# All output products in seven block products for eight, raw products on quarters of the array, one ring of PSUM banks, and a new order of the steps

## The chip, the cores and the metric

The kernel runs on one core of one Trainium2 chip. The metric is the device time of one execution in microseconds; a smaller number is better. Five engines work side by side on their own queues: TensorE (PE in the profile, with its weight loads as PEld), VectorE (DVE), ScalarE (ACT), GpSimd (POOL) and SyncE (SP, which here only issues transfers). Each works through its own instructions in order and waits for semaphores of the others. TensorE writes its results to PSUM, a memory of eight banks that hold 128 x 512 numbers of four bytes each; VectorE and ScalarE carry them on.

## The reference

There are 8 batches, 8 heads, 576 tokens and a head size of 64, so that the heads side by side make 512 channels. First comes an attention without softmax, whose result is normalised over each head; then a gated unit whose gate is a causal convolution over five tokens.

```python
kv = np.einsum('bhsd,bhse->bhde', k, v)
out = np.einsum('bhsd,bhde->bhse', q, kv)
rms = np.sqrt(np.mean(out * out, axis=-1, keepdims=True) + 1e-06)
x = (out / rms * g_norm)                  # then (B,H,S,D) -> (B, S, H*D)
...
for k in range(5):
    gate_pre += conv_w[k] * xp[:, k:k + S, :]     # xp: x with four rows of zeros ahead
gate = 1.0 / (1.0 + np.exp(-gate_pre))
val = x @ w_val
return (gate * val @ w_out).astype(np.float32)
```

The three weights `w_val`, `conv_w` and `w_out` arrive as 64-bit numbers; the rest has 32 bits. All products on TensorE are in 32 bits, and each of them appears in the profile as two instructions ("passes").

## The kernel before

The program is written as small functions ("steps"), and a long string `PLAN` says in which order they are recorded: "raw_pair 3 1; keep_out 0 2; ...". Each step records its instructions on one engine, and since every engine works in order, this string fixes the order on every engine's queue and on the queues of transfers. Semaphores are put in between by the recording layer.

For each batch b the steps are these; a chunk c is 128 tokens, with four whole chunks and a tail of 64 (c = 4).

- **k^T v.** `load_half` brings k and v, `kv_product` (L431) multiplies them in 64 x 64 quarters of the array, four at a time, `kv_copy` (L443, ScalarE) puts the result as blocks on the diagonal of `kv_bd`, 128 x 128 for each pair of heads, the rest of which is zero.
- **q.** For batches 0 and 1 `turn_q_rows` transposes q on TensorE and `sort_q` copies it on ScalarE; later ones are transposed in blocks of 32 x 32 by VectorE (`turn_q`).
- **Raw products.** `raw_product` (L483) multiplies whole tiles of 128 with `kv_bd` for batches 0 and 1 and for all tails; `raw_pair` (L500) takes two whole chunks of batches 2 to 7 in quarters of 64 x 64.
- **Normalising.** `square` (L524, ScalarE), `sums` (L533, VectorE), `powers` (L543, GpSimd, to the power −1/2). For two chunks of batch 0 `roots` (L550) computes the root on VectorE by Newton steps. `normalise` (L564) multiplies: on VectorE for batch 0, on ScalarE, head by head, for the others.
- **x transposed.** Batches 0 and 1 and the tails: `turn_x` on TensorE, `keep_x` on ScalarE. Whole chunks of later batches: `turn_blocks` on VectorE, then `move_blocks`, four transfers each from GpSimd's queue. `halo` on GpSimd copies the four earlier tokens for the convolution.
- **Gate.** For each quarter of the channels `gate_start` (ScalarE), four times `gate_tap` (L623, VectorE), `gate_end` (sigmoid, ScalarE).
- **Values.** Batches 0 and 1 by `val_product` (four products of 288 tokens). From batch 2 on by `val_fast`: a product of two by two blocks in seven block products in place of eight, with sums of blocks of x (`x_sums`) and of weights (`val_sums`) made by VectorE, and `val_keep` to put the parts together. `gated` (L648, VectorE) multiplies by the gate.
- **Output.** Two batches go together as i = b // 2. Batches 0 to 3 (i = 0, 1) go by `out_product` (L712): four products of 128 tokens by 512 columns for each chunk, then `keep_out` (ScalarE). Batches 4 to 7 (i = 2, 3) go by seven block products for each pair p of chunks: `token_sums` (L743) and `weight_sums` make sums of blocks on VectorE, `fast_product` (L761) multiplies (128 tokens by 256 columns, two products each), `fast_keep` (L788) adds the parts up, four copies on ScalarE and three additions on VectorE. `store` sends 128 tokens out in four transfers. All tails go by `out_product` (c = 8).
- **Weights.** `stage_weight` loads, and `narrow_weight` makes 32 bits out of 64 in eight operations, five on VectorE and three on ScalarE.

`start_warm` and `keep_warm` are products whose results nobody reads. PSUM is divided up (L238 to L245): two banks `raws` for k^T v and for most raw products, one bank "tp" for transposes, five banks "mm" for the rest; near the end `raws` is given up for two banks "ends".

Of the kernel before, what the change touches and what calls it, by code (L numbers as in the profile page):

```python
# [9 lines left out]
FP32 = mybir.dt.float32  # L10
# [5 lines left out]
P = 128  # L16
# [3 lines left out]
load_q_rows 0 1; stage_weight cw 0; load_q_rows 0 0; load_half v 0 0; load_half k 0 0; load_half v 0 1;  # L20
load_half k 0 1; warm_up; stage_weight wval 1; stage_weight wval 0; start_warm 36; turn_q_rows 0 0;
turn_q_rows 0 1; narrow_weight cw 0 0; turn_q_rows 0 2; narrow_weight cw 0 1; narrow_weight cw 0 2; sort_q 0 0;
turn_q_rows 0 3; sort_q 0 1; turn_q_rows 0 4; narrow_weight cw 0 3; kv_product 0 0; sort_q 0 2;
load_q_rows 1 0; narrow_weight cw 0 4; narrow_weight cw 0 5; load_half k 1 0; sort_q 0 3; narrow_weight cw 0 6;
load_half v 1 0; narrow_weight cw 0 7; sort_q 0 4; load_q_rows 1 1; load_half k 1 1; stage_weight wval 2;
keep_warm 2; kv_product 0 1; stage_weight wval 3; turn_cw; load_half v 1 1; kv_copy 0; keep_cw;
narrow_weight wval 1 0; raw_product 0 3; load_half v 2 0; raw_product 0 2; square 0 3; raw_product 0 4;
sums 0 3; stage_weight wout 0; square 0 2; raw_product 0 1; square 0 4; powers 0 3; sums 0 2;
narrow_weight wval 1 1; sums 0 4; raw_product 0 0; load_half v 2 1; square 0 1; narrow_weight wval 0 0;
narrow_weight wval 0 1; powers 0 2; square 0 0; normalise 0 3; sums 0 1; turn_x 0 3; sums 0 0; keep_x 0 3;  # L30
powers 0 4; normalise 0 2; narrow_weight wval 1 2; narrow_weight wval 1 3; turn_x 0 2; normalise 0 4;
turn_q_rows 1 0; roots 0; keep_x 0 2; narrow_weight wval 0 2; turn_x 0 4; sort_q 1 0; turn_q_rows 1 1;
keep_x 0 4; narrow_weight wval 0 3; normalise 0 1; turn_q_rows 1 2; halo 0; sort_q 1 1; normalise 0 0;
turn_x 0 1; narrow_weight wval 1 4; kv_product 1 0; narrow_weight wval 0 4; keep_x 0 1; sort_q 1 2;
narrow_weight wval 0 5; turn_x 0 0; narrow_weight wval 1 5; narrow_weight wval 0 6; turn_q_rows 1 3;
keep_x 0 0; narrow_weight wval 0 7; gate_start 0 0; turn_q_rows 1 4; narrow_weight wval 1 6; kv_product 1 1;
sort_q 1 3; load_q 2 0; narrow_weight wval 1 7; gate_start 0 1; narrow_weight wval 2 0; val_product 0 0 1;
gate_start 0 2; narrow_weight wval 3 0; sort_q 1 4; load_q 2 1; gate_tap 0 2 3; kv_copy 1; gate_tap 0 0 3;
narrow_weight wval 3 1; raw_product 1 3; narrow_weight wval 2 1; gate_tap 0 1 3; load_half k 2 0;
raw_product 1 2; keep_val 0 0 1; gate_tap 0 0 2; square 1 3; narrow_weight wval 3 2; val_product 0 1 1;  # L40
sums 1 3; square 1 2; gate_tap 0 1 2; powers 1 3; narrow_weight wval 2 2; load_half k 2 1; gate_tap 0 2 2;
narrow_weight wval 2 3; stage_weight wout 2; raw_product 1 1; sums 1 2; narrow_weight wval 3 3;
narrow_weight wval 2 4; raw_product 1 0; keep_val 0 1 1; powers 1 2; square 1 1; narrow_weight wval 2 5;
normalise 1 3; val_product 0 0 0; load_q 2 2; gate_tap 0 0 1; sums 1 1; turn_q 2 0; normalise 1 2; powers 1 1;
turn_x 1 3; narrow_weight wval 3 4; val_product 0 1 0; narrow_weight wval 2 6; keep_x 1 3; load_q 2 3;
narrow_weight wval 3 5; square 1 0; narrow_weight wval 2 7; normalise 1 1; turn_x 1 2; sums 1 0;
raw_product 1 4; gate_tap 0 2 1; stage_weight wout 1; powers 1 0; kv_product 2 0; narrow_weight wout 0 0;
square 1 4; sums 1 4; narrow_weight wout 0 1; narrow_weight wval 3 6; kv_product 2 1; keep_x 1 2; turn_q 2 1;
powers 1 4; normalise 1 0; gate_tap 0 2 0; turn_x 1 1; load_q 3 0; val_product 0 2 1; narrow_weight wval 3 7;
keep_x 1 1; gate_tap 0 1 1; keep_val 0 1 0; narrow_weight wout 0 2; gate_tap 0 1 0; keep_val 0 0 0; turn_x 1 0;  # L50
normalise 1 4; gate_tap 0 0 0; val_product 0 2 0; narrow_weight wout 2 0; narrow_weight wout 0 3; keep_x 1 0;
narrow_weight wout 0 4; kv_copy 2; val_product 0 3 1; turn_q 2 2; keep_val 0 2 1; keep_val 0 2 0; turn_q 2 3;
narrow_weight wout 2 1; load_q 3 1; gate_end 0 0; narrow_weight wout 0 5; turn_x 1 4; narrow_weight wout 0 6;
raw_pair 2 3; keep_val 0 3 1; keep_x 1 4; gated 0 0; narrow_weight wout 2 2; stage_weight wout 3; halo 1;
val_product 1 0 1; narrow_weight wout 0 7; load_q 3 2; square 2 3; square 2 2; sums 2 3;
narrow_weight wout 2 3; sums 2 2; powers 2 3; gate_end 0 1; val_product 1 0 0; narrow_weight wout 1 0;
gate_end 0 2; narrow_weight wout 2 4; gate_start 0 3; gated 0 1; keep_val 1 0 1; narrow_weight wout 2 5;
# [802 lines left out]
```

## Time and profile before

| | before |
|---|---|
| time, median of 3 runs | 313.97 us (313.96 to 314.11) |
| span of the profiled execution | 313.7 us |
| TensorE busy | 302.8 us, 97% |
| VectorE busy | 255.7 us, 82% |
| ScalarE busy | 191.1 us, 61% |
| GpSimd busy | 133.4 us, 43% |
| read from HBM, written | 39.21 MB, 9.44 MB |
| output products of 512 columns, whole chunks (L718) | 128 passes, of 592 ns each |
| gate taps (L625) | 128, of 810 ns each |

The profiled execution's span lies 0.3 us under the median time, so sums made against the span stand for the time with 0.3 us added. A row of the profile names the engine, the line, the operation, what is written from what, how many there are and how long they were busy; "idle before" is how long the engine stood idle ahead of them, with the instruction that ended the wait. Products are pipelined: one of 592 ns starts 429 ns after the one before, and two rows of busy time can overlap. In the chain of what ended last and in the timeline the first number is the start and the second the time taken, in microseconds.

### The profile page before, as it was taken

What the parts mean: (1) busy time and instruction counts of PE and PEld (TensorE: products, weight loads), DVE (VectorE), ACT (ScalarE), POOL (GpSimd) and SP (SyncE); (2) the same over time, 40 slices, a digit from 0 to 9 for tenths busy, and PEclk for the clock granted to TensorE, in tenths of its full rate; (3) what the DMA queues carried; (4) which work ended last, traced back from release to release, by engine and by line L of the source; (5) the groups of instructions that cost most, each with busy time, mean ns of one, the idle gap of its engine ahead of it and who ended that gap; (6) DMA issues with size and microseconds to landing.
All of it is one profiled execution on the core that took longest, in us unless ns stands there. A gap on an engine that the chain in (4) does not pass through costs nothing.

```text
span 313.7 us, 8362 instructions
## 1 busy us (share of the span) xinstructions
PE 302.8 (97%) x3197; PEld 217.6 (69%) x3197; DVE 255.7 (82%) x462; ACT 191.1 (61%) x542; POOL 133.4 (43%) x175
## 2 busy tenths in 40 slices
PE   7978999999999999999999999999999999999993
PEld 7866878777645485757666776587668868888582
DVE  1149899999999969899999899899998999764412
ACT  1457899999485867747685858485773343352120
POOL 3033073435588456666684659265749000000000
PEclk9999999999999999999999999999999999999999
DMA  7999597599677769668966986422335213022322
GB/s 276 377 386 352 149 294 219 173 298 239 186 189 210 210 188 342 196 168 276 270 155 194 251 251 160 118 50 54 100 78 127 58 25 88 0 67 57 89 73 85
DMA packets 26696, 55.50 MB, mean 177 GB/s; under 512 B 6166, under 2 KB 8214, under 8 KB 26656
## 3 DMA queue, kind: packets, MB, share of 16 engines
q1 hardware_dynamic: 22608, 46.61, 49.8%
q0 software_dynamic: 3168, 6.32, 7.9%
q10 hardware_dynamic: 880, 2.03, 1.9%
q8 instruction: 25, 0.41, 0.5%
q14 instruction: 15, 0.12, 0.1%
HBM read 39.21 MB, written 9.44 MB: 155 GB/s over the span
## 4 chain that ended last, share of the span: by engine, by line
PE 85%; ACT 5%; DMA 4%; DVE 2%; SPq 1%; issue 1%; POOL 1%; ACTq 0%; DVEq 0%
PE out L718 18%; PE va L687 15%; PE a L784 8%; PE vc L687 8%; PE cb L784 6%; PE val L637 6%; PE raw L438 5%; PE out L725 5%; PE raw L510 4%; PE vb L687 4%; PE qTps L472 3%; PE raw L493 2%; DMA k<-in_k_dram 2%; DMA qs<-in_q_dram 2%; PE xTps L587 1%; ACT x L572 1%
## 5 line engine op out<-in xcount | busy, mean ns | idle before, releaser
L625 DVE SCALAR_TENSOR_TENSOR gate<-xT,cwT,gate 128x576 f32<-128x576 f32 x128 | 101.0, 810 | 2.1 <-ACT gate L619 1.6
L546 POOL TENSOR_TENSOR rt<-ss,mhalf 128x8 f32<-128x8 f32 (+1 forms) x38 | 65.4, 1728 | 80.7 <-DVE ss L540 77.1
L608 POOL DMA_DIRECT2D xT<-y x96 | 52.8, 556 | 17.4 <-DVE xs L671 6.0
L718 PE MATMUL out<-wout,gv 128*128 128x512 f32 x128 | 57.3, 595 | 0.0
L572 ACT ACTIVATE x<-raw,rt 128x64 f32<-128x64 f32 x252 | 55.3, 369 | 2.2 <-POOL rt L546 1.6
L718 PEld LDWEIGHTS out<-wout,gv 128*128 128x128 f32 x128 | 23.9, 190 | 26.0 <-issue 24.1
L637 PE MATMUL val<-xT,wval 128*128 128x288 f32 x128 | 32.9, 409 | 0.1
L540 DVE TENSOR_REDUCE ss<-sq 128x8 f32<-128x520 f32 (+1 forms) x38 | 23.3, 626 | 8.3 <-ACT sq L528 8.1
L528 ACT ACTIVATE sq<-raw 128x512 f32<-128x512 f32 (+1 forms) x40 | 21.6, 564 | 12.4 <-PE raw L510 8.8
L637 PEld LDWEIGHTS val<-xT,wval 128*128 128x128 f32 x128 | 23.6, 190 | 6.3 <-ACT xT L594 0.3
L619 ACT ACTIVATE gate<-xT,cwT 128x576 f32<-128x576 f32 x32 | 25.2, 796 | 4.0 <-DVE gv L650 3.9
L687 PE MATMUL va<-xs,vsum 128*128 128x288 f32 x96 | 27.2, 406 | 0.0
L650 DVE TENSOR_TENSOR gv<-gv,gate 128x576 f32<-128x576 f32 x32 | 24.2, 762 | 3.0 <-ACT gate L632 2.8
L632 ACT ACTIVATE gate<-gate 128x576 f32<-128x576 f32 x32 | 22.1, 702 | 5.5 <-DVE gate L625 5.4
L687 PEld LDWEIGHTS va<-xs,vsum 128*128 128x128 f32 x96 | 18.2, 190 | 4.7
L733 ACT COPY ot<-out 128x512 f32<-128x512 f32 x20 | 12.0, 603 | 14.0 <-PE out L725 6.0
L438 PEld LDWEIGHTS raw<-v,k 64*64 64x64 f32 x1008 | 15.5, 135 | 4.7 <-issue 3.8
L793 DVE TENSOR_TENSOR ot<-cb,ot 128x256 f32<-128x256 f32 x16 | 6.7, 420 | 14.7 <-ACT ot L797 7.0
L615 POOL COPY xT<-xT 128x124 f32<-128x124 f32 x32 | 13.4, 456 | 10.3 <-ACT xT L594 10.3
L708 ACT COPY gv<-va 128x288 f32<-128x288 f32 x12 | 4.8, 400 | 19.8 <-PE va L687 19.8
L438 PE MATMUL raw<-v,k 64*64 64x64 f32 x1008 | 16.8, 220 | 0.0
L600 DVE STREAM_TRANSPOSE y<-x 128x512 f32<-128x512 f32 x24 | 16.7, 698 | 0.0
(119 smaller groups left out, 516.7 us busy)
## 6 DMA issues: line engine op xcount, KB each, us to landing
qs<-in_q_dram SPq DMA_DIRECT2D x96, 140.0 KB, 4.3
out_dram<-ot SPq DMA_DIRECT2D x140, 64.0 KB, 2.3
k<-in_k_dram SPq DMA_DIRECT2D x14, 576.0 KB, 6.5
v<-in_v_dram SPq DMA_DIRECT2D x12, 576.0 KB, 6.3
xT<-y POOLq DMA_DIRECT2D x96, 64.0 KB, 3.4
y<-in_moe_w_val_dram SPq DMA_DIRECT2D x4, 512.0 KB, 12.0
w_wout<-in_moe_w_out_dram SPq DMA_DIRECT2D x4, 512.0 KB, 7.2
qs<-in_q_dram SPq DMA_DIRECT2D x3, 576.0 KB, 5.4
```

The lines of the kernel that those rows point to most:

```text
L438: nc.tensor.matmul(raws[r * D:(r + 1) * D, s, i * D:(i + 1) * D], st["k", b, i][rows, r, cols], st["v", b, i][rows, r, cols], start=(j == ...
L540: nc.vector.reduce_sum(out=ss[:, 0:n], in_=st["sq", b, c][:, 0:n], axis=AX.X)
L546: nc.gpsimd.tensor_tensor(out=rt[:, 0:n], in0=st["ss", b, c][:, 0:n], in1=mhalf[:, 0:n], op=ALU.pow)
L572: nc.scalar.activation(out=x[:, to * D:(to + 1) * D], in_=one, func=AF.Copy, scale=st["rt", b, c][:, h:h + 1])
L608: nc.gpsimd.dma_start(out=xTs[b % 2][i * TB:(i + 1) * TB, :, first:first + P], in_=y[a * TB:(a + 1) * TB, i])
L619: nc.scalar.activation(out=gate[:], in_=xTs[b % 2][:, jt, HALO:SX], func=AF.Copy, scale=cwT[:, K - 1, jt:jt + 1])
L625: nc.vector.scalar_tensor_tensor(out=gate[:], in0=xTs[b % 2][:, jt, tap * TB:tap * TB + S], scalar=cwT[:, tap, jt:jt + 1], in1=gate[:], op ...
L637: nc.tensor.matmul(val[:], wval[:, kc, jt * P:(jt + 1) * P], xTs[b % 2][:, kc, HALO + n * SV:HALO + (n + 1) * SV], start=(kc == 0), stop=( ...
L650: nc.vector.tensor_tensor(out=both, in0=both, in1=st["gate", b, jt][:], op=ALU.mult)
L687: nc.tensor.matmul(st[bank, "val", b, mj][:], weights_[:, k], tokens()[:, k], start=(n in (0, 1, 3) and k == 0), stop=(k == NK // 2 - 1), ...
L718: nc.tensor.matmul(po[:], gv[:, jt, first:first + P], wout[:, jt, :], start=(jt == 0), stop=(jt == NK - 1),)
L784: nc.tensor.matmul(st[bank, i, p], tokens()[:, k], weights_[:, k], start=(n < 2 and k == 0), stop=(k == NK // 2 - 1), skip_group_check=True)
```

## The change

Output products of all batches now go by `token_sums`, `fast_product` and `fast_keep`; `out_product` is left for the tails. In `fast_keep` the additions of the banks "b" and "c" are one of 512 columns (n = 5) in place of two of 256 (n = 3 and 5). All raw products, tails too, go by quarters of 64 x 64, each row half into a bank of its own, two banks for a pair of chunks; k^T v is kept as 64 x 64 blocks side by side (`kvs`), with no block diagonal to be zeroed. `square` and, on VectorE, `normalise` therefore work on two halves. Sums and roots of a batch lie in one tile, one power can take several chunks of batch 0, and `roots` is gone. PSUM is one ring of eight banks, k^T v included, and the banks of a block product are asked for when they are first written. `keep_warm` is gone.

The order is new throughout. Among what moves: `start_warm 36` stands behind the raw products of batch 0 in place of the very start; `warm_up` (the sigmoid's table) stands behind three steps of ScalarE; blocks 1, 3 and 2 of w_val are loaded in that order, block 0 behind batch 1's q; batch 1's k^T v stands behind the first `gate_start` in place of ahead of it; blocks 1, 0 and 3 of w_out are loaded ahead of batch 2's q. The block products of the second pairs of batch 3 (i = 1, p = 2, 3) stand behind those of batch 4 (i = 2, p = 0, 1). Behind the last `gated` there remain two pairs of chunks, a tail and some parts of an earlier pair.

```diff
-    BANKS = {"tp": 1, "mm": 5}
-    raws = early.enter_context(tc.tile_pool(name="raws", bufs=1, space=bass.MemoryType.PSUM)).tile(
-        [P, 2, C], FP32, tag="raw", bufs=1, name="raw")
...
-        return psum.tile(shape, FP32, tag=kind, bufs=BANKS[kind], name=name)
+        return psum.tile(shape, FP32, tag="bank", bufs=8, name=name)
...
-    kv_bd = [const.tile([P, HP, P], FP32, name=f"kvbd{i}") for i in range(2)]
+    kvs = [const.tile([P, HP, D], FP32, name=f"kv{i}") for i in range(2)]
...
+        if ("kvps", b) not in st:
+            st["kvps", b] = [ps([P, 2, D], f"kvps{b}_{s}") for s in range(2)]
...
-    def kv_copy(b):
-        for r in range(2):
-            rows = slice(r * D, (r + 1) * D)
-            nc.scalar.copy(
-                out=kv_bd[b % 2][rows, :, rows].rearrange("p (i s) e -> p s i e", s=2),
-                in_=raws[rows, :, 0:2 * D].rearrange("p s (i e) -> p s i e", i=2))
+    def kv_copy(b, s):
+        nc.scalar.copy(out=kvs[b % 2][:].rearrange("p (i s) e -> p s i e", s=2)[:, s], in_=st["kvps", b][s][:])
...
+    def raw_product(b, *chunks):
+        banks = [ps([P, len(chunks), C // 2 if chunks[0] < NJ else P], f"raw{b}_{chunks[0]}_{r}") for r in range(2)]
+        for n, c in enumerate(chunks):
+            st["raw", b, c] = [bank[:, n] for bank in banks]
         for hp in range(HP):
+            for c in chunks:
+                for half in range(2) if c < NJ else (hp // 2,):
+                    first = c * P + (half * D if c < NJ else 0)
                     for r in range(2):
                         rows, cols = slice(r * D, (r + 1) * D), slice(half * D, (half + 1) * D)
+                        to = hp if c < NJ else hp % 2
                         nc.tensor.matmul(
+                            st["raw", b, c][r][cols, to * D:(to + 1) * D],
+                            st["qT", b][rows, hp, first:first + D], kvs[b % 2][rows, hp, :],
+                            start=True, stop=True)
+    def raw_pair(b, c):
+        raw_product(b, c, c - 1)
+    def raw_tail(b):
+        raw_product(b, NJ)
...
+        for r, raw in enumerate(st["raw", b, c]):
+            nc.scalar.activation(
+                out=sq[:, r * n // 2:(r + 1) * n // 2, 0:D], in_=raw.rearrange("p (h e) -> p h e", e=D),
+                func=AF.Square)
...
+    ROOTS = {(0, 2): H + H // 2, (0, 1): 2 * H}
+    def root_range(b, c):
+        return slice(FIRST[c], FIRST[c] + ROOTS.get((b, c), heads(c)))
     def powers(b, c):
+        which = root_range(b, c)
         nc.gpsimd.tensor_tensor(
+            out=st["rt", b][:, which], in0=st["ss", b][:, which], in1=mhalf[:, which], op=ALU.pow)
-    def roots(b):
...
-        if n == 0:
-            for name in "acb":
-                st[name, "val", b, mj] = ps("mm", [P, SV], f"v{name}{b}_{mj}")
+        if n in (0, 1, 3):
+            st[bank, "val", b, mj] = ps([P, SV], f"v{bank}{b}_{mj}")
...
+        if bank == "a" and n == 0:
+            st["a", i, p] = ps([P, C // 2], f"a{i}_{p}")[:]
+        elif bank != "a" and ("c", i, p) not in st:
+            both = ps([P, 2, C // 2], f"cb{i}_{p}")
+            st["b", i, p], st["c", i, p] = both[:, 0], both[:, 1]
+            st["bc", i, p] = both
...
-        elif n == 3:
-            add(first[:, LOW], b)
         elif n == 4:
             add(second[:, HIGH], a)
         elif n == 5:
-            add(first[:, HIGH], c)
+            add(first[:], st["bc", i, p][:].rearrange("p r c -> p (r c)"))
```

## The prediction

> **What bounds the kernel now.** I read the page first, then stretches of busy time, then the chain that ended last, then the timeline of the head.
>
> ```profile
> span 313.7 us, 8362 instructions
> ...
> PE 302.8 (97%) x3197; PEld 217.6 (69%) x3197; DVE 255.7 (82%) x462; ACT 191.1 (61%) x542; POOL 133.4 (43%) x175
> ...
> PEclk9999999999999999999999999999999999999999
> ```
>
> TensorE is busy almost throughout, but busy time is padded by its pipeline, so I take prices from start-to-start times: 0.216 us for a 256-column pass, 0.243 for 288, 0.429 for 512. Added up in the order of the program these prices give 298.7 us; the first product starts at 1.4 us and the last ends at 309.0. At every last `gated` of a batch the sum runs 8 to 9 us behind the clock, so TensorE loses nothing after the head: it is the bound. The next view is busy time by stretches (columns PE, PEld, DVE, ACT, POOL).
>
> ```profile
> 40.00:110.00 70.00, 69.61 (x859) 46.51 (x860) 68.86 (x121) 58.53 (x182) 40.79 (x41) 1.00 0.78 224
> 110.00:200.00 90.00, 90.00 (x1178) 59.60 (x1171) 81.85 (x139) 62.36 (x191) 58.14 (x78) 1.00 0.77 222
> ...
> 35.30:288.70 253.40, 253.01 (x2543) 177.97 (x2543) 232.31 (x390) 168.11 (x497) 125.74 (x159) 1.00 0.59 167
> 288.70:313.70 25.00, 20.05 (x88) 14.01 (x86) 6.74 (x15) 4.18 (x11) 0.00 (x0) 1.00 0.32 85
> ```
>
> VectorE stands close behind: 98.4% busy from 40 to 110 us (68.86 of 70) while TensorE was held up nowhere, and 91.7% from its first gate tap (35.3) to its last `gated` (288.7). The chain gives the prices of whole steps, in time order.
>
> ```profile
> 13.68 1.91 PE warm L429 x4
> ...
> 86.15 10.50 PE out L718 x24
> 96.65 1.09 PE raw L510 x64
> 97.74 0.59 PE raw L493 x8
> ...
> 112.49 1.09 PE raw L510 x64
> 113.58 1.17 PE vc L687 x4
> 114.75 0.97 PE va L687 x4
> ...
> 131.86 3.43 PE out L718 x8
> ...
> 286.91 1.73 PE a L784 x8
> ```
>
> And the head, where the three powers follow the three first sums, and the first gate starts at 32.47:
>
> ```profile
> 6.21 6.25 PE L472 MATMUL qTps<-ident,qs 128*64 128x128 f32 x72 [0.80 <-DMA qs<-in_q_dram]
> ...
> 21.16 4.26 POOL L546 TENSOR_TENSOR rt<-ss,mhalf 128x8 f32<-128x8 f32 x3 [18.00 <-DVE ss L540]
> ...
> 27.46 1.97 PE L472 MATMUL qTps<-ident,qs 128*64 128x128 f32 x32
> ...
> 32.47 0.78 ACT L619 ACTIVATE gate<-xT,cwT 128x576 f32<-128x576 f32 x1
> ...
> 36.81 1.95 PE L493 MATMUL raw<-kvbd,qT 128*128 128x128 f32 x16
> ```
>
> **TensorE, part by part.** *Out products.* A chunk of 128 tokens takes 3.43 to 3.50 us (10.50/3), two chunks 6.9. Seven block products at 0.87 (1.73/2) take 6.1. Eight pairs of chunks change over: 16 x 3.46 = 55.4 becomes 56 x 0.87 = 48.9, a gain of 6.5. *Raw products.* A pair of whole chunks costs 1.95 by full tiles (batches 0 and 1) and 1.09 to 1.12 by quarters: 8 x 0.98 = 7.8 becomes 4 x 1.12 = 4.5. The eight tails cost 0.59 each; by quarters only two of four quarters work at a time, so between a quarter of 1.09 (0.27) and 0.59, in the middle 0.45: 4.8 becomes 3.6. Together 4.5. *Filler in k^T v.* 1.9 goes; `start_warm` (3.9) stays but moves from before q's arrival into the wait for the first roots. *Changes of tile shape.* A product after a change takes 1.17 instead of 0.97 for the way in and out, 0.1 for each; runs of one shape go from 68 to 77: 0.9 more. The sum falls from 298.7 to 285.8 + 0.9.
>
> **The head.** By the order, k^T v's second half still waits for its k, which landed at 13.2. ScalarE then has three q sorts, two k^T v copies and a second table load (1.28, a row of before; there it lay before any data) ahead of the raw products: they start at about 16.4 instead of 17.66. Their squares and first sum end near 18.8. `roots` on VectorE (9 operations of 0.175 and two more, 1.9 us) is gone; GpSimd now takes all 36 columns of batch 0. Three powers with 20 columns took 4.26, 0.21 per column, so 7.7 us, to 26.5. Two normalises in halves (1.4), turn (0.6), keep (0.6) and one operation ahead in ScalarE's queue put the first `gate_start` at 30.0, between 29 (no queue) and 32.5 (no gain). VectorE's taps begin at 30.7. Weights don't hold this: before, wval landed at 14.8 and 16.3, and the order asks for blocks 1, 3 and 2 in that place, ahead of batch 1. Batch 1's q, k and v and the fourth block, seven loads at the 1.5 us that one took before, follow on SyncE's queue behind 17.8 and are in at 28.3, in time for batch 1's k^T v, which now stands behind the first `gate_start`; three blocks of w_out moved ahead of batch 2's q end at 32.8, where its first load had its issue at 33.65.
>
> Behind the first `gate_start` stood 274.2 us of TensorE work in the order (298.7 − 24.5), now 266.7 (285.8 − 20.0 + 0.9). Before, 32.5 + 274.2 = 306.7 against a real 309.0: 2.3 of small waits, which I keep. After the last product the span had 4.7 more (copy, store, landing). So 30.0 + 266.7 + 2.3 + 4.7 = 303.7, and 304.0 as a time, since the median of 313.97 lies 0.3 above the profiled span.
>
> **VectorE.** `token_sums` for two more pairs of batches: 16 x 0.68 = 10.9. `fast_keep`: its adds were 24 x 0.42 = 10.1; now there are 16 of 256 columns (0.42) and 16 of 512 (0.69, as other 512-column operations out of PSUM): 17.8, so 7.7 more. `roots` −1.9, zeroing of the block diagonals −1.0, normalise in halves +0.6. Total 255.7 + 16.3 = 272.0. About 19.7 of it now stand ahead of the first tap (batch 0's sums and normalises, three weight blocks, part of a fourth) and 5.4 behind the last `gated`, leaving 246.9 between. Behind the last `gated`, TensorE has 15.8 in the order plus 1.0, as before (20.3 for 19.3). At the 98.4% of the 40 to 110 stretch VectorE alone gives 30.7 + 246.9/0.984 + 16.8 + 4.7 = 303.1: level with TensorE. Two engines that level don't both run without waiting. By the order, up to batch 1's third `gated` VectorE has 67.9 us of start-to-start work where TensorE has 68.2; at the 4% idle of that phase before (62.1 for 59.6) it comes about 3 us late there, and I let half of this reach TensorE, as those products are asked for some 7 us later: +1.5. **305.5.**
>
> **Others.** ScalarE gets 64 + 16 half squares (0.42 and some 0.3) for 40 whole ones, +10, more out copies of 0.37, +2.3, and the table load: 191 to about 204, 67% of the span, hidden while its work isn't what releases a bank. GpSimd's and SyncE's instructions are as many as before: 96 block moves, 140 stores; DMA was 59% busy over the middle, so I price their moved places at nothing; if that cover fails, a store (2.3 us to land) holds an out tile, of which there are still three.
>
> [...] The 72 passes at 6.21 took 87 ns each, the 32 at 27.46 took 62: start-to-start 207 ns per two up to 10.5 us, 106 after, although PEclk reads full. The small fillers from 1.4 to 5.2 hadn't brought the faster pace. [...]
>
> **Rivals.** (1) *VectorE keeps the share it has now*, 91.7%, since it waits for banks, roots and copies whatever TensorE does. Place: first tap to last `gated`. 30.7 + 246.9/0.917 + 16.8 + 4.7 = 321.4, as a time 321.7: slower. It decides from 94.4% down, where the gain is gone. For it: 110 to 200 us had 90.9%. Against: there TensorE was the one that was full. In between, 95 to 97% gives 307 to 312. (2) *Banks.* Raw products hold two banks until a whole pair is normalised, and one ring serves all. In the compiled order 172 reuses of a bank stand where 121 stood; half have at most 2.6 us of TensorE work between the last reader and the next writer (6.8 before), and 17 at most 1.0. If each of those 17 waits between nothing and half a normalise on ScalarE (8 x 0.2 us / 2 = 0.8), it costs 0 to 14; in the middle 311. (3) *The head is shorter and the planned order has no waits*: 29 + 266.7 + 0.8 + 4.7 + 0.3 = 301.5, and 300 if the tails run four abreast. (4) That block products aren't cheaper, because each needs its own weight load: before, a load took 190 ns and a pass 216, so it hid; excluded.
>
> **How the numbers follow.** Forecast, 302 to 309: 0.52. Rival 1: 0.21, of it 0.11 above 314. Rival 2: 0.17, of it 0.03 above 314. Rival 3: 0.10. What a measurement can tell from no change is 0.2%, 0.6 us: within 313.3 to 314.6 I put 0.02; faster 0.84, slower 0.14. The range from 300 to 314 leaves out the far half of rival 1 and little else; the likeliest case's own range is 302 to 309.
>
> **What would show it.** The group of 512-column out products is gone, block products come twice as often at 0.216 start to start; raw products are all quarters, tails at 0.3 to 0.6 us; VectorE near 272 us busy, 97% between first tap and last `gated`; first `gate_start` near 30; two table loads. Wrong: idle time on TensorE behind 30 us beyond 5 us in total. If it is ended by ScalarE's normalise or copies, rival 2; if by VectorE's turns, token sums or taps, rival 1.

## The result, and the profile after

The changed kernel takes 332.71 us (median of 4 runs, 330.86 to 334.45) where the kernel before took 314.04 on the same chip (313.96 to 315.05): 1.0585 times as long, 95% interval 1.0532 to 1.0638. It is slower by 5.9%, and 27 us above the forecast. Times here are medians of all runs of a kernel; the ratios leave out runs that lay over 1.5% above the kernel's fastest. The page of the profiled execution has it in four lines and one row of transfers:

```profile
span 332.3 us, 9138 instructions
...
PE 300.8 (91%) x3545; PEld 235.5 (71%) x3545; DVE 269.9 (81%) x478; ACT 193.0 (58%) x599; POOL 136.5 (41%) x175
...
PEclk9967999999995999999997997999999999999998
...
q8 instruction: 28, 0.46, 0.6%
...
PE 55%; DMA 13%; DVE 11%; issue 7%; ACT 5%; POOL 4%; SPq 3%; DVEq 0%; POOLq 0%; ACTq 0%
```

TensorE is no longer busy throughout, the granted clock falls at four places (to 0.50 in the stretches below) where the page of the kernel before has it full all along, and in the chain that ended last (the last line) transfers have 13% and "issue", an engine waiting for nothing that the profile shows, 7%. (From here on a "product" is one line of the profile, that is, one pass.) The q8 row will matter: its 28 packets, of 16 KB each (0.46 MB in all), go by their number with TensorE's instructions. TensorE had 3,545 products and 3,545 weight loads, 7,090, so 253 for each packet. Before there were 25 packets for 6,394, one for 256; e9 below has 27 for 6,946, one for 257. So in these runs a packet of 16 KB goes with about 256 of TensorE's instructions.

The view of waits, TensorE alone, names where it stood (total, how often, longest):

```profile
PE qTps L468 <- DMA qs<-in_q_dram: 6.4, 1, 6.4
PE vb L652 <- DMA xT<-y: 6.0, 1, 6.0
PE raw L492 <- issue: 3.8, 2, 3.2
PE out L690 <- issue: 3.1, 1, 3.1
PE va L652 <- ACT sq L512: 2.6, 1, 2.6
```

The first is the start. The second is batch 2's `val_fast`, which waits for moved blocks of x. The third and fourth have no releaser: one lies within batch 0's raw products (L492), one within the out product of a tail (L690). The fifth is put down to a `square`, but the last block move of batch 4 landed at 173.69 and TensorE went on at 173.99: it is x again.

The stretches between, with what follows each wait (busy time of PE, PEld, DVE, ACT, POOL, then granted clock, DMA share, GB/s):

```profile
18.55:28.79 10.24, 7.01 (x183) 6.71 (x172) 6.31 (x14) 5.83 (x15) 6.29 (x3) 0.50 1.04 396
30.00:97.37 67.37, 67.37 (x1126) 54.23 (x1122) 64.62 (x115) 57.63 (x174) 29.52 (x33) 1.00 0.66 185
97.37:103.37 6.00, 0.00 (x0) 0.03 (x1) 1.57 (x3) 1.59 (x5) 4.30 (x4) 0.76 1.04 264
103.37:107.29 3.92, 3.92 (x8) 2.84 (x9) 1.36 (x2) 0.00 (x0) 0.00 (x0) 0.50 0.58 175
171.37:173.99 2.62, 0.00 (x1) 0.03 (x1) 0.08 (x2) 2.14 (x11) 2.05 (x2) 1.00 0.60 149
175.56:178.97 3.41, 3.40 (x128) 3.40 (x132) 3.38 (x6) 0.78 (x4) 2.27 (x2) 0.50 0.70 184
200.51:203.59 3.08, 0.01 (x1) 0.00 (x1) 2.97 (x5) 1.23 (x3) 1.35 (x4) 0.88 0.63 138
203.59:206.28 2.69, 2.69 (x8) 1.15 (x9) 0.42 (x1) 0.00 (x0) 2.02 (x4) 0.50 0.36 90
```

From 30 to 97 us TensorE is full, as forecast. Then come three waits of 6.00, 2.62 and 3.08 us, and with each a stretch at a clock of 0.50, 6.83, 3.41 and 3.41 us long. Two of these stretches set in before the wait is over, 2.90 and 0.72 us ahead of its end (the clock of 0.76 and 0.88 in the rows of the waits); the one that goes with the wait of 2.62 us sets in 1.6 us behind it. While the first wait lasts, the DMA engines are full (1.04).

And the head, by its timeline:

```profile
17.88 3.19 PE L492 MATMUL raw<-kv,qT 64*64 64x64 f32 x128 [0.57 <-issue]
...
24.30 0.69 PE L492 MATMUL raw<-kv,qT 64*64 64x64 f32 x12 [3.23 <-issue]
...
24.92 4.02 PE L428 MATMUL warm<-ident 128*32 128x32 f32 x72
...
28.87 1.97 PE L468 MATMUL qTps<-ident,qs 128*64 128x128 f32 x32
...
37.07 1.45 ACT L585 ACTIVATE gate<-xT,cwT 128x576 f32<-128x576 f32 x2
```

128 quarter products run, TensorE stands for 3.2 us, the last 12 follow, then 4 us of filler, and the first `gate_start` comes at 37.07, 7.1 us behind the forecast.

**The sum.** The forecast for a profiled span was 305.2, the span is 332.3. Of the 27.1: 7.1 in the head; 13.8 in idle stretches of TensorE of over 0.7 us behind it (the three waits and two of 0.7 and 0.9, each counted as what a start came later than its usual distance); 5.0 by the clock, an estimate (13.7 us at a clock of 0.50 behind the head, 3.6 of them idle, so some 10 us of work; a product of 288 columns started 480 ns after the one before at 0.50 and 243 at 1.00, so half of the 10 us counts as lost); 1.2 is left.

### The profile page after: what moved, and what is told of

It reads as the page before. It is cut to its first block, busy times and chain, and to the rows that moved or that the text cites. A ratio compares the mean times of both kernels' runs of the same rounds, so it can differ in the third digit from the quotient of the medians.

```text
span 332.3 us, 9138 instructions
## 1 busy us (share of the span) xinstructions
PE 300.8 (91%) x3545; PEld 235.5 (71%) x3545; DVE 269.9 (81%) x478; ACT 193.0 (58%) x599; POOL 136.5 (41%) x175
## 4 chain that ended last, share of the span: by engine, by line
PE 55%; DMA 13%; DVE 11%; issue 7%; ACT 5%; POOL 4%; SPq 3%; DVEq 0%; POOLq 0%; ACTq 0%
PE val L603 9%; PE a L744 8%; DMA xT<-y 8%; PE cb L744 7%; PE va L652 7%; DVE gate L591 5%; PE vc L652 4%; PE raw L492 4%; PE kvps L438 3%; PE qTps L468 3%; PE vb L652 3%; PE out L690 3%; POOL xT L574 3%; DMA qs<-in_q_dram 3%; DMA out_dram<-ot 2%
## 5 line engine op out<-in xcount | busy, mean ns | idle before, releaser
L529 POOL TENSOR_TENSOR rt<-ss,mhalf 128x8 f32<-128x8 f32 (+3 forms) x38 | 67.5, 1780 | 95.2 <-DVE ss L521 95.0
L512 ACT ACTIVATE sq<-raw 128x256 f32<-128x256 f32 (+1 forms) x80 | 24.7, 379 | 17.7 <-PE raw L492 14.8
L744 PE MATMUL a<-wsum,sums 128*128 128x256 f32 x128 | 32.7, 381 | 0.0
L492 PEld LDWEIGHTS raw<-kv,qT 64*64 64x64 f32 x1152 | 20.3, 141 | 12.5 <-issue 9.0
L492 PE MATMUL raw<-kv,qT 64*64 64x64 f32 x1152 | 23.6, 230 | 4.9 <-issue 3.8
L744 PEld LDWEIGHTS a<-wsum,sums 128*128 128x128 f32 x128 | 23.9, 190 | 3.5
L438 PEld LDWEIGHTS kvps<-v,k 64*64 64x64 f32 x1008 | 17.8, 146 | 4.6 <-issue 2.8
L652 PE MATMUL vb<-xT,wval 128*128 128x288 f32 x48 | 15.0, 438 | 6.4 <-DMA xT<-y 6.0
L438 PE MATMUL kvps<-v,k 64*64 64x64 f32 x1008 | 19.6, 232 | 0.6 <-ACT x L541 0.5
L690 PE MATMUL out<-wout,gv 128*64 128x512 f32 x64 | 16.9, 644 | 3.1 <-issue 3.1
```

The costliest lines, as they stand in the source:

```text
L438: nc.tensor.matmul(st["kvps", b][s][r * D:(r + 1) * D, i], st["k", b, i][rows, r, cols], st["v", b, i][rows, r, cols], start=(j == 0), sto ...
L492: nc.tensor.matmul(st["raw", b, c][r][cols, to * D:(to + 1) * D], st["qT", b][rows, hp, first:first + D], kvs[b % 2][rows, hp, :], start=T ...
L529: nc.gpsimd.tensor_tensor(out=st["rt", b][:, which], in0=st["ss", b][:, which], in1=mhalf[:, which], op=ALU.pow)
L652: nc.tensor.matmul(st[bank, "val", b, mj][:], weights_[:, k], tokens()[:, k], start=(n in (0, 1, 3) and k == 0), stop=(k == NK // 2 - 1), ...
L690: nc.tensor.matmul(po[r * T:(r + 1) * T], gv[:, jt, first:first + T], wout[:, jt, :], start=(jt == 0), stop=(jt == NK - 1),)
L744: nc.tensor.matmul(st[bank, i, p], tokens()[:, k], weights_[:, k], start=(n < 2 and k == 0), stop=(k == NK // 2 - 1), skip_group_check=True)
```

## The experiments

Theories after the result: **(A)** the x moves of a batch now run beside the loads of k and v for the batch after next, and land late; **(B)** TensorE runs out of instructions in long runs of quarter products (a "stop" below is a stretch in which TensorE stands and the profile names no releaser); **(C)** a wait costs a second time, by the clock; **(D)** the filler lies on the path. Rivals from the prediction: VectorE's share, and banks. In the table "idle" is TensorE's idle stretches of over 0.7 us behind 36 us in the profiled execution, reckoned as above; ratios are to the kernel before on the same chip. "First `gate_start`" and "idle" belong to one execution, which is not always a typical one: it took 328.64 us in e6, 319.49 in e9, 321.10 in e10, 318.48 in e11 and 321.94 in e14, 2 to 5 us over the median, and 332.21 in e4, 4 us under it. The same head gave a first `gate_start` between 35.74 and 37.30 (the changed kernel, e2, e4, e5, e6), so in that column 1.5 us says nothing by itself.

| run | time, us | ratio, 95% interval | first `gate_start` | idle |
|---|---|---|---|---|
| changed kernel | 332.71 | 1.0585, 1.0532 to 1.0638 | 37.07 | 13.8 |
| e1 no filler | 328.26 | 1.0432, 1.0373 to 1.0492 | 33.76 | 14.6 |
| e2 batch 4's loads late | 329.01 | 1.0470, 1.0404 to 1.0536 | 36.16 | 10.0 |
| e3 quarters spread | 333.36 | 1.0613, 1.0547 to 1.0680 | 36.24 | 12.5 |
| e4 fill, long | 336.32 | 1.0640, 1.0554 to 1.0727 | 35.74 | 7.2 |
| e5 fill, short | 330.42 | 1.0505, 1.0441 to 1.0569 | 36.10 | 8.7 |
| e6 loads of 6, 7 early | 323.61 | 1.0271, 1.0217 to 1.0326 | 37.30 | 8.1 |
| e7 all of these | 317.84 | 1.0101, 1.0070 to 1.0133 | 34.92 | 2.8 |
| e8 before, 4 block pairs | 345.53 | 1.0995, 1.0903 to 1.1088 | 32.43 | 25.4 |
| e9 as e7, own head | 316.62 | 1.0042, 1.0008 to 1.0076 | 34.84 | 4.4 |
| e10 e9 + start filler | 318.11 | 1.0100, 1.0036 to 1.0164 | 34.65 | 4.9 |
| e11 e9, three taps | 316.61 | 1.0010, 0.9978 to 1.0043 | 34.34 | 6.1 |
| e12 e9, batch 0 full tiles | 314.52 | 0.9999, 0.9976 to 1.0022 | 31.16 | 3.4 |
| e13 e9, 4 pairs direct | 324.79 | 1.0343, 1.0302 to 1.0384 | 35.02 | 6.7 |
| e14 e12, three moves | 319.87 | 1.0114, 1.0076 to 1.0152 | 31.71 | 6.7 |

**e1: the filler.**

```diff
-start_warm 36; narrow_weight wval 1 7;
+narrow_weight wval 1 7;
```

> The only edit: the 36 small filler products behind batch 0's raw products are gone. Theory 'filler on the path': in the changed kernel they ran from 24.92 to 28.94 while batch 1's q products and the turn of x stood behind them in TensorE's order. Without them those start near 25, VectorE gets its x tiles back about 2.5 us earlier, and the first gate_start comes near 34.3 instead of 37.07, held from there on by the third root (ends at 30.0). Time 332.7 - 2.7 = 330.0, ratio 1.050 to before. Theory 'filler is covered': first gate_start stays at 37, time 332 to 333, ratio 1.058. The idle stretches behind 90 us stay in both.

It was on the path: `gate_start` at 33.76 (34.3 expected), time 4.4 us less (2.7 expected), and the two intervals don't overlap. The filler had been recorded as harmless cover for the wait for roots; but batch 1's q products and the turn of x stand behind it in the order.

**e2: the loads beside batch 2's moves.**

```diff
-load_half v 4 0; load_half k 4 0; load_q 4 0; load_half k 4 1; load_half v 4 1; raw_pair 3 1;
+load_q 4 0; raw_pair 3 1;
...
+store 0 3; load_half v 4 0; load_half k 4 0; load_half k 4 1; load_half v 4 1;
```

> The only edit: the four loads of batch 4's k and v (576 KB each) stand behind the stores of out tile 0 3 on SyncE's queue instead of ahead of them, so that they no longer run beside the 16 block moves of batch 2. Theory 'the moves collide with the loads': issue to landing of a move falls from a median near 6 to 2.5 us, the last moves land near 101 instead of 105.7, TensorE's wait of 6.0 us for x of batch 2 falls to 1.5 to 3, and the stretch at lower clock behind it goes: 332.7 - 3 to 4.5 - 1.7 = 326.5 to 328, less up to 2 us that k^T v of batch 4 may wait for its later loads. Theory 'the moves come late by themselves' (VectorE's turns of the batch and GpSimd's queue set them): wait stays at 5.5 to 6, time 332 to 334.

Issues and their median time to landing, 86 to 106 us, first of the changed kernel, then of e2 (number of issues, KB each, us):

```profile
v<-in_v_dram SPq DMA_DIRECT2D x2, 576.0 KB, 8.7
k<-in_k_dram SPq DMA_DIRECT2D x2, 576.0 KB, 9.5
xT<-y POOLq DMA_DIRECT2D x16, 64.0 KB, 7.0
```

```profile
v<-in_v_dram SPq DMA_DIRECT2D x2, 576.0 KB, 5.7
k<-in_k_dram SPq DMA_DIRECT2D x2, 576.0 KB, 5.5
xT<-y POOLq DMA_DIRECT2D x16, 64.0 KB, 3.3
```

Both sides of the collision are seen: moves 7.0 against 3.3 us, loads 9 against 5.6. TensorE's wait fell from 6.0 to 1.1 and the time by 3.7. That is less than the 4.9 of idling and some 2 of slow work that went, because a new stop without a releaser appeared in batch 4's k^T v; its waits view:

```profile
...
PE va L652 <- ACT ot L767: 3.2, 1, 3.2
PE out L690 <- issue: 2.9, 1, 2.9
PE kvps L438 <- issue: 2.2, 1, 2.2
...
PE vb L652 <- DMA xT<-y: 1.1, 1, 1.1
```

Theory A holds for this wait by the trace; the interval of the time just touches the changed kernel's (1.0536 against 1.0532).

**e3: shorter runs of quarter products.**

```diff
-raw_pair 0 3; raw_tail 0; raw_pair 0 1;
+raw_pair 0 3; raw_tail 0; start_warm 36; raw_pair 0 1;
...
-kv_product 7 0; out_product 1 8;
+out_product 1 8; kv_product 7 0;
```

> Two moves in TensorE's order: the filler now stands between the two raw pairs of batch 0, and the first k^T v half of batch 7 stands behind the out product of the tail rows instead of ahead of it, so that no long run of 64x64 products is left at these two places. Theory 'TensorE runs out of instructions after some 130 dense quarter products': both idle stretches without a releaser (3.23 us at 21.07, 3.08 us at 200.51) vanish, with the lower clock behind them (0.56 in 20 to 30 us, 0.83 in 200 to 210). In the head the filler then costs about what the gap did, so there is 0.8 to 2.7 us gained there; 3.1 + 1.4 at the tail product. Time 332.7 - 5.3 to 7.2 = 325.5 to 327.5. Theory 'the gaps belong to what else happens at these times' (loads on all DMA engines in the head): a gap of 3 us stays at 21 or at 200 us, and time stays above 329.

The stops are gone from both places, but not the time. Its waits view:

```profile
PE vb L652 <- DMA xT<-y: 7.8, 2, 4.9
...
PE warm L428 <- issue: 1.6, 1, 1.6
```

This is far from the 325.5 to 327.5 expected. The x wait now happens twice: 4.9 us at batch 2 as before, and 2.9 us at 202 for batch 5's x, which the stop in the tail product had been hiding. In the head the stop moved into the filler (1.6). What a stop costs is not what its disappearance gives.

**e4 and e5: a filler in the wait.**

```diff
+fill 50;   (e4; in e5: fill 28)
 val_fast 2 1 3;
```

> The only edit: 50 filler products of 128 columns (some 5.5 us) ahead of the first block product of batch 2's val, in the place where TensorE waited 6.0 us. Theory 'the wait costs twice, once as idling and once as a lower clock after it': the granted clock from 100 to 110 us is 1.00 instead of 0.66, the first 36 val products take 9.0 to 9.4 us instead of 11.0, and the time falls by 1.7 to 2.2 to 330.5 to 331, ratio 1.053. Theory 'the slow products are late x blocks, sums or banks': they take 11 us again, and the time stays at 332 to 333.

> The longer filler before took 193 ns for each product and overran the wait; now 28 of them, 5.4 us, stand ahead of the first block product of batch 2's val. Theory 'the wait costs twice': the first val product still starts near 103, the granted clock from 100 to 110 us is 1.00 instead of 0.66, the first 36 val products take 9.0 to 9.3 us instead of 11.0, and the time falls by about 2, to 330.5. Theory 'the slow products are late data': 11 us again, time 332 to 333.

A filler product of e4 took 193 ns, so 50 of them overran the wait by 3.7 us; the clock was 1.00 from 100 to 110 us. The time rose to 336.32, where theory C had forecast 330.5 to 331 for a filler that ends with the wait. e5 has the wait filled just to its end:

```profile
97.37:103.37 6.00, 5.95 (x51) 5.76 (x50) 0.60 (x2) 0.62 (x3) 3.73 (x3) 1.00 1.02 261
103.37:107.29 3.92, 3.92 (x17) 3.04 (x17) 2.78 (x5) 2.45 (x12) 0.00 (x0) 1.00 0.39 134
```

In the same 3.92 us TensorE now does 17 products in place of 8, VectorE five operations in place of two. At the pace of the 17 the 8 products would have taken 1.8 us, 2.1 less. Theory C holds by the trace: the wait of 6.0 us cost 8. The time falls by 2.3, but the intervals overlap, and e5's first `gate_start` was 1.0 us earlier as well, so the time alone doesn't show it.

**e6: the loads beside batches 4 and 5's moves.**

```diff
-load_half k 6 0; ... load_half k 6 1; ... load_half v 6 1; ... load_half v 7 0; load_half k 7 1; load_half v 7 1;
+load_half v 6 0; load_half k 6 0; load_half k 6 1; load_half v 6 1;
+load_half k 7 0; load_half v 7 0; load_half k 7 1; load_half v 7 1;
```

(and `kv_product 7 0` as in e3)

> From the changed kernel, with three loads of batch 6 and three of batch 7 earlier on SyncE's queue, ahead of the block moves of batches 4 and 5, and the first k^T v half of batch 7 behind the tail out product. Theory 'moves collide with loads': the waits for x at 171 (2.62 us) and at 202 (3.2 us in the run that spread the quarters) fall below 1 us each, the gap in the tail product (3.08) is gone too, the clock stays at 1.00 behind 150 us: 332.7 - 2.6 - 3.1 - 2 = 325. Theory 'the moves are late by their own chain': one of the waits stays at 2.5 us or more, time 329 to 333.

The time falls by 9.1 us, 7.7 expected. From 150 to 210 us a move lands after a median of 3.1 us in place of 5.8 (first the changed kernel, then e6):

```profile
xT<-y POOLq DMA_DIRECT2D x32, 64.0 KB, 5.8
```

```profile
xT<-y POOLq DMA_DIRECT2D x32, 64.0 KB, 3.1
```

The waits for x at 171 and 202 are gone from the view of waits, and so is the stop in the tail product. The wait for batch 2's x, which this edit doesn't touch, stays (5.4). Theory A holds here too. How much of the 9.1 is the moved loads and how much the moved `kv_product 7 0` was not told apart.

**e7 and e9: all together.** e7 also changes the order of chunks in batch 0's head; there the squares of its chunk 1 replace those of chunk 2 before these are summed, so one chunk's roots are others, at the same instructions. e9 keeps the changed kernel's own order.

```diff
-raw_pair 0 3; raw_tail 0; raw_pair 0 1;
+raw_pair 0 3; raw_pair 0 1; raw_tail 0;   (e7 alone)
```

> All that was found so far in one: no filler; raw pairs of batch 0 ahead of its raw tail, roots in the order 3, then 1 and 0, then 2 and 4; loads of batch 4 late, of batches 6 and 7 early; k^T v of batch 7 behind the tail out product. If the effects add up: 332.7 - 4.4 (filler) - 2 (last root near 28 instead of 30) - 3.7 (batch 4's loads) - 7.7 (batches 6 and 7) = 315, with the first gate_start near 32. If TensorE's waits only move on to the next late transfer or to VectorE, as one did when the quarters were spread: 320 to 325. If the order of the changed kernel holds nothing beyond these waits the sum forecast (305.5) would come into reach only below 310.

> As e7_combo, but the head keeps the changed kernel's order of chunks (3, 2, tail, 1, 0), only without the filler; loads of batch 4 late, of batches 6 and 7 early, k^T v of batch 7 behind the tail out product. In e1 this head gave the first gate_start at 33.76, in e7 it came at 34.92 with 281.2 us behind it. If the parts add up: 33.8 + 281.2 = 315.0, as a time 316.5. If the shorter head only lets the next waits for x come up again: 318 or more.

The effects nearly add up. Alone, e1, e2 and e6 gave 4.4, 3.7 and 9.1 us, 17.2 together; e9 is 16.1 us below the changed kernel. That it met the 316.5 expected is in part luck: its first `gate_start` came 1.0 us later than assumed there. e7 missed its 315 by 2.8 us. The idle stretches behind the head are down from 13.8 to 2.8 (e7) and 4.4 us (e9), and e9's clock is 1.00 from 40 to 300 us. What is left of the 27 us lies elsewhere. In the head e9 reads as the changed kernel did:

```profile
17.74 3.06 PE L492 MATMUL raw<-kv,qT 64*64 64x64 f32 x128 [0.54 <-issue]
24.10 0.69 PE L492 MATMUL raw<-kv,qT 64*64 64x64 f32 x12 [3.30 <-issue]
```

**e10: where the stop stands.**

```diff
-turn_q_rows 0 3;
+start_warm 56; turn_q_rows 0 3;
```

> e9 with 56 small filler products at the very start, where TensorE waits for q. They put 224 more instructions ahead of the raw products. In all runs so far TensorE stood still some 128 quarter products into batch 0's raw products, and went on 1.3 to 1.6 us after a 16 KB piece of its instructions had come in. Theory 'the pieces have a fixed size and come at a fixed place of the instruction list': the place moves forward by 224 instructions, so the gap no longer stands near the 66th of 71 pairs of raw products but behind some 20 of them or is gone from the raw products; if it is covered by the earlier start, first gate_start 31 to 32 and time 2 us below e9; if it is only moved, the same time as e9 within 1 us. Theory 'the gap comes from the loads on the DMA engines at that time': it stays at 20.5 to 21.5 us whatever stands ahead.

Its timeline:

```profile
15.18 0.56 PE L492 MATMUL raw<-kv,qT 64*64 64x64 f32 x20 [0.20 <-ACT kv L444]
17.57 2.08 PE L492 MATMUL raw<-kv,qT 64*64 64x64 f32 x124 [1.82 <-issue]
20.15 0.40 PE L468 MATMUL qTps<-ident,qs 128*64 128x128 f32 x3 [0.50 <-DMA qs<-in_q_dram]
23.87 1.54 PE L468 MATMUL qTps<-ident,qs 128*64 128x128 f32 x12 [3.32 <-issue]
```

In the changed kernel TensorE stops behind its 221st product (0.57 us) and its 349th (3.23); in e7 and e9, too, 128 raw products stand between two such stops (1.22 and 2.87 us, 0.54 and 3.30) and 12 behind them. Here, with 112 products put ahead, behind the 223rd, 349th and 476th. The places are fixed in the list of instructions, 126 to 128 products apart, 252 to 256 instructions with the weight loads, about one packet, and what stands ahead decides which work they fall into: the 349th product is the 132nd raw product there and the 20th here. So theory B holds, by position. The times fit as well: in both stops of more than 2 us without a releaser in the changed kernel the trace has a 16 KB packet that starts within the stop, 0.80 and 0.15 us behind its beginning, and TensorE goes on 1.5 and 1.6 us after it has come in (stop from 21.07, packet from 21.87 to 22.80, on at 24.30; stop from 200.51, packet from 200.66 to 202.00, on at 203.59). In the head the packets start about every 6 us (15.65, 21.87 and 28.15 in the changed kernel), and the 128 quarter products between the two stops, 256 instructions, take 3.19. e10 itself gains nothing: the raw products end 5 us earlier, and the stop stands among batch 1's q products instead. (Its time is 1.5 us above e9's, where 1 was expected at most; the intervals overlap.)

**e11: VectorE.**

```diff
-gate_tap 0 3 0; ... gate_tap 7 3 0;   (all 32 with the tap 0; the output lacks that tap)
```

> e9 with one of the four gate taps of each row left out (32 VectorE operations of some 0.83 us, 26.6 us in all; the earliest tap of the convolution is missing from the output). Theory 'VectorE sets what is left behind the first gate_start': with 27 us less on VectorE the time falls by 4 to 7 us below e9. Theory 'it is not VectorE' (TensorE's own order, banks freed by ScalarE, transfers): it falls by less than 1.5 us.

VectorE's busy time falls from 269.5 to 247.8 us. The medians are the same (316.62 and 316.61); the ratios, 1.0042 and 1.0010, differ by 1.0 us, and their intervals overlap. If VectorE set the time, 4 to 7 us less were expected. So VectorE doesn't set what is left in e9.

**e12: batch 0's raw products by full tiles.**

```diff
-raw_pair 0 3; raw_tail 0; raw_pair 0 1;
+raw_full 3; raw_full 2; raw_full 4; raw_full 1; raw_full 0;
...
+    def raw_full(c):
+        ...   as before's raw_product, one bank for a chunk, with a block-diagonal k^T v for batch 0
```

> e9 with one part of the change undone at one place: batch 0's raw products go by full tiles against a block-diagonal k^T v again (36 matmuls for 142 quarter products), the rest stays on quarters. Theory 'in the head TensorE is bound by the supply of its instructions, a piece of 256 every 6 us': although a pair of chunks costs 0.86 us more by full tiles, the gap of 3.6 us inside the raw products goes, they end near 22.5 instead of 24.7, the third root starts some 2 us earlier, the first gate_start comes at 32.5 to 33 instead of 34.84, and the time falls by about 2 to 314.5. Theory 'the gap is only a wait that something else would take over' (roots on GpSimd, turns of x, weights on VectorE): first gate_start stays at 34.5 or above, time 316 to 317.5.

```profile
15.96 5.28 PE L492 MATMUL raw<-kvbd,qT 128*128 128x128 f32 x40 [1.36 <-ACT kvbd L449]
21.17 1.97 PE L476 MATMUL qTps<-ident,qs 128*64 128x128 f32 x32
```

40 products for 144, in one run without a stop; the roots begin at 19.81 and take 7.76 us; the first `gate_start` comes at 31.16, earlier than expected, and the time is 2.1 us less than e9's (the intervals just overlap): 314.52, the same as the kernel before (0.9999, 0.9976 to 1.0022). The clock, too: over the span of the profiled execution it is 0.995 in e12 and 0.980 in e9, whose page has two slices of the head (15.9 to 31.8 us) at 0.6. In this head full tiles are the faster ones, though a pair of chunks costs nearly twice as much by them (1.95 us for 1.09 in the kernel before).

**e13 and e8: what block products are worth.**

```diff
-fast_product 0 0 0; ... fast_product 0 3 6;   (with their sums and adds)
+out_product 0 0; keep_out 0 0; ...            (e13, from e9)
```

> e9 with the other part undone for half of its places: the out products of batches 0 and 1 (four pairs of chunks) by 512-column products again, each at the place of the fourth and the last of its block products; token sums and adds of these pairs are gone from VectorE. By the prediction's prices TensorE gets 4 x 0.82 = 3.3 us more, so 320 if the saving of the block products is real and reaches the time. If the block products give back what they save, by waits for their sums, copies and out tiles: 315 to 317.5, no slower than e9.

e13 is 8.2 us slower than e9 where 3.3 were expected. So the block products don't give back what they save, as the second theory had it. But 8.2 isn't the size of the saving: this order, put together without that work, also has a wait of 2.5 us for x, one of 1.0 for v and a stop of 1.5 without a releaser, which e9 doesn't have. That the 3.3 reach the time in full fits these numbers and isn't shown.

```diff
-out_product 1 0; ... keep_out 1 0; ...         (e8, from before: batches 2 and 3)
+fast_product 1 0 0; fast_product 1 0 1; fast_keep 1 0 0; ...
```

> The kernel before with one part of the change alone: the out products of batches 2 and 3 (four pairs of chunks) in seven block products instead of eight, each pair at one place of the order, its stores behind it; the rest of the order is before's. By the prediction's prices: 4 x (6.92 - 6.1) = 3.3 us less on TensorE, so 310.7 (ratio 0.990) if the gain reaches the time. VectorE gets 8 token sums (5.4 us) and 12 adds of 256 columns (5.1 us) between 150 and 265 us: if it is VectorE that decides there, the time stays at 313 to 317 (ratio 0.998 to 1.010).

e8 is 31 us slower than before, far outside both theories. Its waits views, TensorE and VectorE:

```profile
PE xTps L593 <- ACT x L578: 8.0, 3, 5.8
...
DVE ot L799 <- ACT ot L803: 20.4, 7, 5.6
```

The additions that I put in stand on VectorE ahead of other work and wait 20 us in all for ScalarE's copies. It says nothing on the price of block products, only that they can't be dropped into an order that was not made for them.

**e14: two more single waits.**

```diff
-narrow_weight wval 2 1; keep_x 0 1; gate_start 0 3; gate_start 0 2;
+keep_x 0 1; gate_start 0 3; gate_start 0 2; narrow_weight wval 2 1;
...
-load_q 4 0; ... turn_q 4 0; store 0 3;
+store 0 3; load_q 4 0; ... turn_q 4 0; turn_q 4 3;
```

(In this order the fourth pair of batch 4's rows of q overwrites the first before that is turned, so batch 4's q isn't the input's.)

> e12 with three small moves: one weight operation of ScalarE behind the first gate_start instead of ahead of it (0.71 us on the chain to it), the last load of q that ran beside batch 2's block moves behind them as well, with its turn on VectorE. If what is left is a sum of such small waits: first gate_start near 30.5, the wait for x of batch 2 (1.2 us at 92.5) below 0.5, time 314.5 - 0.7 to 2 = 312.5 to 313.8, ratio 0.994 to 0.998. If other waits take their places: 314 to 315, ratio 1.000.

319.87 us, 1.0114 (1.0076 to 1.0152), slower than e12 and outside both theories, whose times were 312.5 to 313.8 and 314 to 315. In the profiled execution the wait for batch 2's x is gone, and in its place:

```profile
PE kvps L440 <- DMA k<-in_k_dram: 2.8, 1, 2.8
```

Batch 4's k, now queued behind more of q, is late. The first `gate_start` didn't move forward (31.71). In kind it is the second of the two theories: the wait that went made room for another, here a longer one.

## Why the prediction was wrong

**The step that failed first** is in "Others": "DMA was 59% busy over the middle, so I price their moved places at nothing; if that cover fails, a store ... holds an out tile". 59% is a mean over 250 us. In the 6 us that mattered the engines were full (1.04), because the order issues 16 block moves (1 MB) within the same 12 us as four loads (2.3 MB), and what was late was x. The prediction had counted bytes and not when they are asked for. In the kernel before batch 2's last moves were issued from 96.7 to 98.9 us, and TensorE's first product with that x started at 111.3. Here the last move was issued at 98.85, after GpSimd had stood 1.98 and 1.01 us for earlier moves to land, and TensorE was ready for x at 97.4. e2 and e6 take the collision away and give back 3.7 and 9.1 us (e6 with the tail stop).

**The clock stood in no term of the sum.** In the kernel before, TensorE's longest idling behind 6.2 us was 1.33 us, and the page has the clock full; but the question was whether the changed kernel would have longer waits. With gaps of 2.6 to 6 us it cost some 5.0 us behind the head, an estimate, 2.1 of them read from e5's products. In the changed kernel the granted clock was 0.50 in stretches of 3.41, 6.83 and 10.24 us: once it fell after 2.36 us of idling (200.51 to 202.87), once after 3.10 (97.37 to 100.47), once 1.57 us behind a wait of 2.62 us. The forecast priced none of the four places.

**Raw products.** "4 x 1.12 for 8 x 0.98" was right for a pair by itself (1.09 to 1.16). It was wrong for 72 + 144 quarter products with one other between them: 256 instructions were used in 3.19 us where the head brought a packet every 6 (15.65, 21.87, 28.15). No row of before showed this price: its longest such runs, 144 products, stood elsewhere and did not stop. A bound from both sides was missing, and the quarter's price should have been taken per instruction as well as per column.

**The head** (30.0 forecast, 37.07 measured). Right: two table loads, raw products from about 16.4 (16.98), three powers of 7.7 us (7.76 in e12). Wrong: the stop (3.2 us, which puts the third power's end at 30.0 in place of 26.5), and "`start_warm` stays but moves ... into the wait for the first roots": it ran 24.92 to 28.94 with work queued behind it; e1 has the first `gate_start` 3.3 us earlier without it (2.0 to 3.5 against the other runs with this head). Without both, e12 has 31.16, within the range of 29 to 32.5 given there.

**What was right.** Block products start 216 ns apart (median), the group of 512-column products is gone, VectorE is 269.9 us busy (272.0 forecast), ScalarE 193 (204). The test for "wrong" that the prediction named, idle time of TensorE beyond 5 us behind 30 us, is what happened (13.8), though neither of the two enders it named.

**The rivals.** VectorE's share: e11 excludes it for what e9 has left; in the changed kernel the waits of TensorE put down to VectorE are 1.6 us (1.2 and 0.4). Banks: behind 38 us the waits put down to ScalarE and VectorE come to 5.3 us, and 2.6 of these were x; 2.7 us is near the low end of "0 to 14". No rival had transfers of x or the supply of instructions as its mechanism, and 0.84 for "faster" rested on a sum in which both were nothing.

**From span to time.** The 0.3 us that the forecast added was mistaken. In every run on record a time lies 1.73 to 1.86 us above the span of the same execution. So the span of 313.7 belongs to an execution of some 315.5 us, not to the median of 313.97, and the forecast was 1.5 us too low by this step alone. (Two products in its sum are also a little off, 56 x 0.87 is 48.7 and 8 x 0.59 is 4.7; together that moves the sum by 0.1 us.)

**What stays open.** e12 still lies 9 us above the forecast: 1.2 in the head, 6.3 behind it by the profiled spans (281.5 for 275.2), and the 1.5 from span to time. Behind the head TensorE's named waits come to 5.6 us, 1.8 more than allowed, in ten places of 0.2 to 1.2. The rest is products that start a little later than their prices: 225 ns on the mean for 216 (447 passes, 4.0 us), 251 for 243 (336 passes, 2.7), of which 0.9 had been priced. Not all of this is new: in the kernel before the same kinds of passes came 222 (223 passes) and 247 ns apart, 2.9 us over their prices. Which of changes of width, quarter runs ahead of them and the supply of instructions makes these was not told apart. So behind the head e12 spends 281.5 us where the profiled execution of the kernel before spent 281.2: 7.5 us less work by the forecast's sum, and none of it left in the time.

## What to carry to other kernels

When a change moves transfers, look at the stretch from issue to first reader and at what else is issued in the same ten microseconds; a mean DMA share over the middle covers nothing. A product's price has a second part, its instructions: where small tiles come in long runs, count instructions per microsecond against the runs that the profile shows. When TensorE waits as long as it did here (2.62, 3.08 and 6.00 us), price the wait and a stretch at a clock of 0.50 (here 3.41 to 6.83 us of it with each), and expect that the wait may hide a second one.

## What the runs showed of the hardware

- Packets of 16 KB on the queue q8, of the kind "instruction", came at one for 253 to 257 of TensorE's instructions (28 for 7,090 in the changed kernel, 25 for 6,394 before, 27 for 6,946 in e9). In the head of the changed kernel, with the DMA engines full (1.04), they started some 6 us apart (15.65, 21.87, 28.15), and 128 dense 64 x 64 products, 256 instructions, took 3.19 us, most of it at a clock of 0.50; TensorE then stood for 3.23 us, and the profile puts that down to "issue". A stop moved by the number of instructions put ahead of it, from 132 products into the raw products to 20 (e10). At 200 us it also happened with the DMA engines at 0.63. What sets the start of a packet was not tested. Another run of 144 such products, at 88 us in the changed kernel, took 2.33 us without a stop.
- The granted clock in the traces of the kernel before and the changed kernel is 1.00 or 0.50, and between two changes lie 3.41 us or a multiple of it (at 0.50: 10.24, 6.83, 3.41 and 3.41). Within a wait of 6.0 us it fell to 0.50 and stayed there for 3.9 us of the work behind it; 8 products ran in these where 17 ran with the wait filled (e5). Products of 288 columns started 480 ns apart at 0.50 and 243 at 1.00.
- Block moves of 64 KB landed after a median of 7.0 us beside four loads of 576 KB and after 3.3 without them (86 to 106 us, the changed kernel and e2); the loads themselves took 9 for 5.6.
